# Filling the block-diagonal state matrix: copies on GpSimd from rows already on chip, in place of transfers from memory

## The chip, the core and the metric

The kernel runs on one core of a Trainium2 chip. The metric is the device time of one launch in microseconds (us); lower is better. TensorE does matrix products and transposes, VectorE (DVE in the profile), ScalarE (ACT) and GpSimd (POOL) do elementwise work, and SyncE (SP) issues most of the transfers between the main memory and the core's own memory. All five run at the same time, each through a queue of its own in a fixed order, and wait for each other through semaphores.

## What is computed

Three stages follow one another. The change lies in the first; the two others appear here because their time follows from it.

```python
def _attn_ref(x, state):                 # x (8, 8, 512, 64), state (8, 8, 32, 64)
    scores = scale * np.matmul(x, state.transpose(0, 1, 3, 2))
    a = softmax(scores)                  # over the 32 state rows
    xread = np.matmul(a, state)
    scores2 = scale * np.matmul(state, x.transpose(0, 1, 3, 2))
    a2 = softmax(scores2)                # over the 512 rows of x
    sread = np.matmul(a2, x)
    return np.concatenate([xread, sread], axis=2)
# then: each of the 4608 rows goes to the best of 8 experts, relu(x @ w1) @ w2, scaled by two gates
# then: ((x @ w1) * (x @ w2)) @ w3 @ w_out
```

The two softmaxes are written out in the reference (subtract the maximum, exponential, divide by the sum plus 1e-9).

## The kernel before, in words

The attention handles the eight batches one after the other. The four steps that matter here are:

- `load_x(b)` (line 323) brings one batch of x, 1 MB, with four transfers on SP's queue. `load_state` (line 337) brings all state rows into `st_n`, once, at the start: partition 32 j + n holds row n of the heads 2 j and 2 j + 1, 64 numbers each, for all batches.
- `softmaxes(b)` (line 524) makes the scores of a batch and both softmaxes. VectorE takes maxima and sums (lines 556 to 590), ScalarE the exponentials (lines 586 and 602), GpSimd normalises (line 593). ScalarE, or VectorE, copies transposed blocks out of TensorE's result memory (`cp`, lines 138 to 140; "any" in its lists lets the framework choose the engine).
- `read(b)` (line 623) multiplies the softmax weights with the state. It needs a block-diagonal matrix: for four heads at once, the rows of head j stand in partitions 32 j to 32 j + 31 and in columns 64 j to 64 j + 63, everything else is zero. That is `st_d` (line 373), for four batches at a time and for even and odd heads (g); 32 columns behind hold gate products (`spread_gates`, line 376). Its products are `pxr` (line 654).
- `load_w_out` and `load_w3` bring weights for a later stage as raw 64-bit words and convert them (`convert`, line 211): ScalarE line 225, VectorE 228, 230 and 233, ScalarE 239, GpSimd 240, in this order. Of w_out's blocks (`wu_raw`) three are loaded at the start.

`st_d` is cleared once by GpSimd (line 374). `spread_state(b, n)` (line 381) fills in the rows of n batches. It is called for batches 0 to 3 at the start (line 391), and for two batches each after `read(1)` and `read(3)` (lines 675 and 686), when the products with the old rows are through. Each call issues eight transfers, one for each head, on the queue that `q_std` names in the list KN: SP's. One moves 32 rows for n batches, in runs of 256 bytes: 32 KB in the first call, 16 KB in the two others.

The order of instructions in each queue is not written by hand. The framework lays out the whole program on an estimated timeline when the kernel is built (line 1570), and each engine takes, of the instructions that are ready by that estimate, the one with the highest priority. Priority follows the program's order, with offsets for the attention's steps:

```python
"u": lambda b: ([(load_w_out(i), split_w_out()) for i in WU[b]]),
"r": lambda b: (read(b), b % 2 == 1 and b < B // 2 and spread(b + B // 2 - 1, 2)),
# KN: 'order': 'xswrguf'; prio for x s u r g w f: 0, 300, 0, 300, 0, -300, 0
```

After the attention the logits of all rows give the routing (`route`, line 728); the experts' rows are gathered and their weights loaded by what it decides, and TensorE works through the experts and the last stage.

Of the kernel before, what the change touches and what calls it, by code (L numbers as in the profile page):

```python
# [52 lines left out]
def tile_attention_moe_bilinear(  # L53
# [20 lines left out]
    nc = tc.nc  # L74
    B, H, S, D = x.shape
    NS = state.shape[2]
# [6 lines left out]
    NJ = H // 2  # L83
# [4 lines left out]
    def kn(name, default):  # L88
        return KN.get(name, default)
# [43 lines left out]
    def eng(name, i, default="any"):  # L133
        v = kn(name, default)
        v = v[i % len(v)] if isinstance(v, list) else v
        return getattr(nc, v)
# [49 lines left out]
    def both(t, *at):  # L186
        return t[0][at], t[1][at]
# [122 lines left out]
    with ExitStack() as c1:  # L310
# [12 lines left out]
        def load_x(b):  # L323

            t = xin.tile([P, H, NC_, D], F32, tag="x", name=f"x{b}")
            for j in range(NJ):
                h = slice(2 * j, 2 * j + 2)
                eng("q_x", j, "sync").dma_start(
                    out=t[:, h].rearrange("p h c d -> p h (c d)"),
                    in_=x[b, h].rearrange("h (p c) d -> p h (c d)", c=NC_),  # L330
                )
            x_t[b] = t


        st_n = one.tile([P, B, 2 * D], F32, name="st_n")
# [33 lines left out]
        nc.scalar.dma_start(out=wg[:, :, 0:E], in_=w_gate.rearrange("(k p) e -> p k e", p=P))  # L369
        nc.scalar.dma_start(out=wg[:, :, E:], in_=w_ogate.rearrange("(k p) e -> p k e", p=P))  # L370
        load_x(1)

        st_d = one.tile([P, B // 2, 2, NJ * D + 2 * E], F32, name="st_d")
        nc.gpsimd.memset(st_d, 0.0)
# [4 lines left out]
                nc.gpsimd.tensor_copy(st_d[:, i : i + n, g, NJ * D :], st_g[:, g, b : b + n])  # L379

        def spread_state(b, n):
            for h in range(H):
                j, g = divmod(h, 2)
                i = b % (B // 2)
                eng("q_std", h, "gpsimd").dma_start(
                    out=st_d[NS * j : NS * (j + 1), i : i + n, g, j * D : (j + 1) * D],
                    in_=state[b : b + n, h].rearrange("b n d -> n b d"),
                )

        load_x(2)  # L390
        spread_state(0, B // 2)


        stT = [one.tile([P, B, P], F32, name=f"stT{o}") for o in range(2)]
        for i in range(0, B, 4):
# [6 lines left out]
            for o in range(2):  # L402
# [4 lines left out]
                        turned[:, j].rearrange("p g d -> p (g d)") if o else st_n[:, i + j, :], ident,  # L407
                    )
                nc.vector.tensor_copy(stT[o][:, i : i + 4, :], t.rearrange("p (j n) -> p j n", j=4))

        def of(g):
            return slice(D * g, D * (g + 1))

        def at(j):
            return slice(NS * j, NS * (j + 1))


        st_g = one.tile([P, 2, B, 2 * E], F32, name="st_g")
# [1 line left out]
        def gate_state():  # L420
            t = [bank((kn("t_psg", "C")*4)[0], f"psg{g}")[:, 0 : B * 2 * E] for g in range(2)]
            for b in range(B):
                for j in range(NJ):
                    for g in range(2):
                        nc.tensor.matmul(
                            t[g][at(j), b * 2 * E : (b + 1) * 2 * E], stT[0][of(g), b, at(j)],
                            wg[of(g), j, :], start=True, stop=True,
                        )
            for g in range(2):
                nc.vector.tensor_copy(st_g[:, g], t[g].rearrange("p (b e) -> p b e", e=2 * E))  # L430
# [93 lines left out]
        def softmaxes(b):  # L524
# [20 lines left out]
            for j in range(NJ):  # L545
                for g in range(2):
                    for e in range(2):
                        nc.tensor.matmul(
                            t[e][at(j), g * S // 2 : (g + 1) * S // 2], stT[e ^ g][of(e), b, at(j)],
                            xT[of(e), 2 * j + g, :], start=True, stop=True,  # L550
                        )
# [123 lines left out]
        def spread(b, n):  # L675
            spread_state(b, n)
            spread_gates(b, n)
# [213 lines left out]
    with ExitStack() as c2:  # L891
# [446 lines left out]
        for n, c in enumerate(ORDER):  # L1338
            if c != "b":
                b = [n + 1] if ORDER[n + 1 : n + 2] == "b" else []  # L1340
# [178 lines left out]
    with tc.If(used > T0):  # L1519
        with ExitStack() as c6:  # L1520
            e2 = Lines(c6.enter_context(tc.tile_pool(name="e2_more", bufs=2, reuse_waits="tile")))
            e4 = Lines(c6.enter_context(tc.tile_pool(name="e4", bufs=2, reuse_waits="tile")))
            n = MAXT - T0
# [50 lines left out]
```

## Time and profile before

| what | value |
|---|---|
| median of 3 runs | 1165.69 us (1165.29 to 1167.22) |
| the profiled execution's own time | 1171.04 us |
| its span, first to last instruction | 1169.1 us |
| TensorE's mean granted clock in it | 0.99 |
| busy in the span: TensorE, VectorE, ScalarE, GpSimd | 1118.7, 664.0, 450.7, 398.2 us |
| transfers of the span | 211.55 MB |

Times of rows count from the start of the span. In a timeline a row reads: start, duration (both us), engine and line, operation, written <- read tensors (buffer numbers left out), shapes, how many instructions the row merges, and in brackets how long the engine was idle before and what ended that. SPq is SyncE's queue of transfer issues: the duration there is the issuing, not the transfer itself.

### The profile page before, as it was taken

How to read it: one execution, taken by the hardware profiler on the slowest of the kernel's cores; microseconds unless marked ns; L12 is line 12 of the kernel's file. 1: busy time of each engine (PE TensorE's matmuls, PEld its weight loads, DVE VectorE, ACT ScalarE, POOL GpSimd, SP SyncE). 2: the span in 40 equal slices, each digit the busy share in tenths (PEclk: the TensorE clock that was granted, in tenths of full speed). 3: DMA queues.
4: the chain of work that ended last, by engine and by line, in shares of the span. 5: the costliest groups of instructions: out<-in, count | busy, mean ns of one | idle time of the engine just before them, and what ended most of it. 6: DMA issues, size and time to landing. Idle time of an engine off the chain costs nothing. (4 is left out here: it accounts for less than half of the span.)

```text
span 1169.1 us, 18224 instructions
## 1 busy us (share of the span) xinstructions
PE 1118.7 (96%) x6880; PEld 982.7 (84%) x6880; DVE 664.0 (57%) x1206; ACT 450.7 (39%) x807; POOL 398.2 (34%) x383
## 2 busy tenths in 40 slices
PE   6888998999999999999999999999999999999995
PEld 4666777999999999987888888898888889889994
DVE  4999787636464546464855547343644545463341
ACT  3778644435454545454413223121412322131121
POOL 2555326114140322132001434623543453344222
PEclk9899999999999999999999999999999999999998
DMA  7786425546566666677414645443544445343431
GB/s 227 223 254 200 160 96 209 201 153 228 187 228 211 215 216 201 233 221 242 158 35 176 248 152 199 171 174 141 205 174 160 156 180 189 135 181 132 184 127 57
DMA packets 85008, 211.55 MB, mean 181 GB/s; under 512 B 12976, under 2 KB 42672, under 8 KB 79920
## 3 DMA queue, kind: packets, MB, share of 16 engines
q1 hardware_dynamic: 62256, 167.53, 42.2%
q10 hardware_dynamic: 17024, 24.42, 5.7%
q0 software_dynamic: 5632, 18.35, 4.5%
q8 instruction: 56, 0.92, 0.3%
q14 instruction: 40, 0.33, 0.1%
HBM read 166.23 MB, written 44.04 MB: 180 GB/s over the span
## 5 line engine op out<-in xcount | busy, mean ns | idle before, releaser
L183 PE MATMUL p<-w_x,w 128*128 128x448 f32 (+1 forms) x1638 | 338.6, 360 | 0.0
L183 PEld LDWEIGHTS p<-w_x,w 128*128 128x128 f32 x1638 | 303.7, 188 | 25.4
L183 PE MATMUL py<-h,w 128*128 128x288 f32 (+1 forms) x1152 | 197.9, 329 | 3.0 <-ACT y L1087 3.0
L183 PE MATMUL ph<-x,w 128*128 128x288 f32 (+2 forms) x1248 | 196.5, 316 | 2.9 <-DVE h L1025 2.7
L183 PEld LDWEIGHTS ph<-x,w 128*128 128x128 f32 x1248 | 179.4, 188 | 15.6 <-DVE h L1025 4.4
L183 PEld LDWEIGHTS py<-h,w 128*128 128x128 f32 x1152 | 173.8, 188 | 19.2 <-ACT y L1087 4.6
L178 DVE TENSOR_TENSOR w<-raw,w 128x1024 fp32r<-128x1024 f32 x80 | 96.9, 1237 | 74.6 <-ACT w L177 72.5
L1434 POOL TENSOR_TENSOR ab<-u,s 128x448 f32<-128x448 f32 (+1 forms) x40 | 47.6, 1189 | 259.3 <-DVE u L1432 170.4
L183 PE MATMUL po<-w_wo,aa 128*128 128x512 f32 x480 | 125.3, 393 | 1.9 <-ACT aa L177 1.0
L183 PEld LDWEIGHTS po<-w_wo,aa 128*128 128x128 f32 x480 | 89.7, 188 | 18.8 <-DVE aa L178 1.7
L177 ACT CAST w<-raw 128x1024 fp32r<-128x1024 f32 x80 | 81.6, 1050 | 51.6 <-DMA raw<-in_moe_w 46.8
L177 ACT CAST ab<-ab 128x384 fp32r<-128x384 f32 (+1 forms) x40 | 19.7, 493 | 184.4 <-POOL ab L1440 174.0
L240 POOL TENSOR_TENSOR wab<-wab,wab_top 128x512 int32<-128x512 int32 x16 | 20.7, 1292 | 179.5 <-DVE wab_top L233 151.5
L183 PE MATMUL po<-w_wo,ab 128*128 128x512 f32 x336 | 79.6, 391 | 0.4 <-DVE o L1466 0.4
L183 PEld LDWEIGHTS po<-w_wo,ab 128*128 128x128 f32 x336 | 62.9, 188 | 13.9 <-DVE o L1466 0.8
L997 POOL DMA_INDIRECT xg<-x_rows,gidx x38 | 45.7, 1202 | 83.3 <-PE pxg L1003 66.7
L1437 DVE TENSOR_TENSOR u<-u,p 128x448 f32<-128x448 f32 (+1 forms) x40 | 24.3, 606 | 84.4 <-PE p L183 84.3
L1438 POOL TENSOR_TENSOR ab<-u,s 128x448 f32<-128x448 f32 (+1 forms) x40 | 48.3, 1208 | 49.2 <-DVE u L1437 49.2
L1025 DVE SCALAR_TENSOR_TENSOR h<-ph,h 128x288 fp32r<-128x288 f32 (+2 forms) x104 | 51.2, 502 | 20.8 <-ACT h L1024 20.3
L1024 ACT ACTIVATE h<-ph 128x288 fp32r<-128x288 f32 (+2 forms) x104 | 44.5, 447 | 42.6 <-PE ph L183 30.8
L183 PE MATMUL pwo<-wu,w3T 128*128 128x512 f32 x192 | 50.2, 411 | 3.4 <-POOL w3T L178 2.9
L1440 POOL TENSOR_TENSOR ab<-ab 128x448 f32<-128x448 f32 (+1 forms) x40 | 48.9, 1222 | 3.1
(291 smaller groups left out, 1441.0 us busy)
## 6 DMA issues: line engine op xcount, KB each, us to landing
w<-w_rows SPq DMA_DIRECT2D x39, 1792.0 KB
raw<-in_moe_w SPq DMA_DIRECT2D x80, 512.0 KB
x<-in_x SPq DMA_DIRECT2D x32, 256.0 KB
w_raw<-in_moe_w SPq DMA_DIRECT2D x16, 512.0 KB
x_rows<-xr SPq DMA_DIRECT2D x32, 256.0 KB
w_rows<-wh_s ACTq DMA_DIRECT2D x32, 256.0 KB
y<-y_T SPq DMA_DIRECT2D x8, 896.0 KB
w_rows<-wh_w ACTq DMA_DIRECT2D x32, 192.0 KB
```

Of the source, the lines that this page charges most:

```text
L177: nc.scalar.copy(hi, src)
L178: (engine or nc.vector).tensor_tensor(lo, src, hi.bitcast(F32), op=ALU.subtract)
L183: m = nc.tensor.matmul(o, l[a], r[b], start=start and i == 0, stop=stop and i == 2)
L240: nc.gpsimd.tensor_tensor(wi, wi, top, op=ALU.add)
L997: gathered = nc.gpsimd.indirect_dma_start(out=x[0:r], out_offset=None, in_=x_rows, in_offset=bass.IndirectOffsetOnAxis(ap=gidx[0:r, t - s0 ...
L1024: nc.scalar.activation(hl[0], src, AF.Relu)
L1025: nc.vector.scalar_tensor_tensor(out=hl[1], in0=src, scalar=0.0, in1=hl[0].bitcast(F32), op0=ALU.max, op1=ALU.subtract)
L1434: gpsimd(b2, u3, s5, op=ALU.add)
L1437: vector(u4, u2, p3, op=ALU.add)
L1438: gpsimd(a2, u4, s5, op=ALU.add)
L1440: gpsimd(ab[:, n : 2 * n], a2, b2, op=ALU.mult)
```

## The change

`spread_state` issues no transfers any more. For each of the four partition blocks GpSimd copies the rows of both heads (g = 0 and 1) of n batches out of `st_n`, which is loaded at the start anyway, into the diagonal blocks of `st_d`: four copies a call in place of eight transfers, twelve in place of 24 in all. A copy has 32 partitions and n x 2 x 64 elements in each. The helpers `of` and `at` move up so that they are defined.

```diff
         st_d = one.tile([P, B // 2, 2, NJ * D + 2 * E], F32, name="st_d")
         nc.gpsimd.memset(st_d, 0.0)
...
         def spread_state(b, n):
-            for h in range(H):
-                j, g = divmod(h, 2)
-                i = b % (B // 2)
-                eng("q_std", h, "gpsimd").dma_start(
-                    out=st_d[NS * j : NS * (j + 1), i : i + n, g, j * D : (j + 1) * D],
-                    in_=state[b : b + n, h].rearrange("b n d -> n b d"),
+            i = b % (B // 2)
+            for j in range(NJ):
+                nc.gpsimd.tensor_copy(
+                    st_d[at(j), i : i + n, :, j * D : (j + 1) * D],
+                    st_n[at(j), b : b + n, :].rearrange("p b (g d) -> p b g d", g=2),
                 )
```

## Rows read from the trace of the kernel before

**Rows 1.** Busy time of each engine by stretch: start:end, engines, granted clock, transfers
```profile
0.00:30.00 30.00, 18.41 (x296) 14.40 (x300) 13.83 (x41) 10.50 (x18) 8.21 (x35) 0.95 0.75 221
30.00:125.00 95.00, 83.09 (x910) 59.35 (x903) 94.47 (x250) 74.23 (x158) 53.19 (x45) 0.96 0.74 227
125.00:1169.10 1044.10, 1017.23 (x5688) 908.97 (x5686) 555.73 (x918) 365.93 (x632) 336.76 (x304) 0.99 0.50 176
```

**Rows 2.** Timeline of ScalarE, 15 to 30 us
```profile
15.90 0.72 ACT L602 ACTIVATE a<-sT,nm 128x512 f32<-128x512 f32 x1 [4.04 <-DVE nm L600]
...
19.32 1.06 ACT L586 ACTIVATE a<-a 128x1024 f32<-128x1024 f32 x1
26.21 0.66 ACT L225 ACTIVATE wu_top<-wu_raw 128x512 f32<-128x512 f32 x1 [5.83 <-DMA wu_raw<-in_moe_w_out]
...
28.58 1.06 ACT L140 COPY a2T<-pa2T 128x512 f32<-128x512 f32 x2
```

**Rows 3.** Timeline of VectorE, 26 to 29 us
```profile
26.90 0.43 DVE L228 TENSOR_SCALAR wu_top<-wu_top 128x512 f32<-128x512 f32 x1 [3.90 <-ACT wu_top L225]
27.25 0.17 DVE L589 TENSOR_SCALAR s<-s 128x32 f32<-128x32 f32 x1
28.16 0.43 DVE L228 TENSOR_SCALAR wu_top<-wu_top 128x512 f32<-128x512 f32 x1 [0.73 <-ACT wu_top L225]
```

**Rows 4.** Timeline of SP's queue, 10 to 21 us
```profile
10.78 5.79 SPq L385 DMA_DIRECT2D st_d<-in_state  x8
...
19.14 1.41 SPq L208 DMA_DIRECT2D wu_raw<-in_moe_w_out  x3
```

**Rows 5.** Waits of SP's queue up to 21 us: total us, times, longest
```profile
SPq L385 <- DMA x<-in_x: 3.5, 8, 0.6
```

**Rows 6.** Stretches as in rows 1; the last three columns: clock, transfer engines' share, GB/s
```profile
15.00:18.50 3.50, 3.50 (x69) 2.92 (x61) 3.13 (x13) 2.48 (x6) 0.00 (x0) 1.00 0.39 69
18.50:26.00 7.50, 4.73 (x51) 3.01 (x49) 3.98 (x12) 1.58 (x2) 0.43 (x2) 1.00 0.97 336
...
28.00:37.00 9.00, 7.15 (x83) 5.90 (x84) 8.85 (x18) 6.35 (x14) 5.48 (x4) 0.50 0.54 142
```

**Rows 7.** GpSimd's copies in the first 30 us by shape: total us, mean ns
```profile
L399 POOL COPY turned<-st_n 128x256 f32<-128x256 f32 x4 | 1.5, 405 | 0.4 <-DMA wg<-in_moe_w_gate 0.4
...
L379 POOL COPY st_d<-st_g 128x64 f32<-128x64 f32 x2 | 0.4, 238 | 9.1 <-DVE st_g L430 9.1
```

**Rows 8.** Timeline of all engines, 5 to 9 us
```profile
6.48 1.09 POOL L399 COPY turned<-st_n 128x256 f32<-128x256 f32 x3
...
8.51 0.85 PE L405 MATMUL pst<-ident,turned 128*128 128x128 f32 x3
```

**Rows 9.** Timeline of all engines, 54 to 56 us
```profile
54.34 0.68 DVE L233 SCALAR_TENSOR_TENSOR wu_top<-wu_raw,wu_top 128x512 int32<-128x512 int32 x1
...
55.16 1.27 POOL L240 TENSOR_TENSOR wu<-wu,wu_top 128x512 int32<-128x512 int32 x1 [3.29 <-ACT wu_top L225]
55.18 1.53 DVE L228 TENSOR_SCALAR wu_top<-wu_top 128x512 f32<-128x512 f32 x1
```

**Rows 10.** VectorE's groups by shape, 30 to 125 us: total us, mean ns, idle before
```profile
L233 DVE SCALAR_TENSOR_TENSOR w_top<-w_raw,w_top 128x512 int32<-128x512 int32 x13 | 11.7, 904 | 0.0
...
L228 DVE TENSOR_SCALAR w_top<-w_top 128x512 f32<-128x512 f32 x14 | 8.6, 612 | 0.0
...
L228 DVE TENSOR_SCALAR wu_top<-wu_top 128x512 f32<-128x512 f32 x6 | 4.7, 781 | 0.0
...
L606 DVE TENSOR_SCALAR r<-s 128x2 f32<-128x2 f32 x6 | 3.5, 586 | 0.0
L589 DVE TENSOR_SCALAR s<-s 128x32 f32<-128x32 f32 x6 | 3.4, 569 | 0.0
```

**Rows 11.** Copies of line 140, 30 to 125 us: ns min/median/max, first and last start
```profile
L140 ACT COPY xT<-pxT x16: 560/580/653, 36.3 to 118.3; 128x512 f32<-128x512 f32 x16
...
L140 DVE COPY xT<-pxT x8: 665/676/692, 36.0 to 117.9; 128x512 f32<-128x512 f32 x8
```

More of the change, by code (lines that the diff above doesn't have):

```diff
@@ L371, in tile_attention_moe_bilinear, with of, at @@
         load_x(1)
+        def of(g):
+            return slice(D * g, D * (g + 1))
+        def at(j):
+            return slice(NS * j, NS * (j + 1))
         st_d = one.tile([P, B // 2, 2, NJ * D + 2 * E], F32, name="st_d")
@@ L409, in tile_attention_moe_bilinear @@
                 nc.vector.tensor_copy(stT[o][:, i : i + 4, :], t.rearrange("p (j n) -> p j n", j=4))
[L411 to L415, printed above, removed]
         st_g = one.tile([P, 2, B, 2 * E], F32, name="st_g")
```

## The prediction, written before the result

> **What bounds the kernel now.** I read the stages first: busy time of each engine over the first 30 us, the next 95 us and the rest [rows 1]. The reader should see three different limits. From 125 us to the end TensorE is busy 1017.23 of 1044.10 us; nothing the change touches lies there, so what the start gains is handed on to the end, because routing, gathers and expert weights all wait for the last logits. From 30 to 125 us VectorE is busy 94.47 of 95.00 us, and ScalarE (74.23) and GpSimd (53.19) are not: VectorE alone sets that stage. In the first 30 us nobody is full, and VectorE works 13.83 us: that stage is bound by waits.
>
> So I looked for the wait that ends last there, in time order on ScalarE [rows 2]. ScalarE stands idle 5.83 us, up to 26.21, for the first raw block of w_out; its two conversion pairs come ahead of the copies of a2T in its queue, and those copies start at 28.58 only. VectorE follows: idle 3.90 us up to 26.90 and 0.73 us up to 28.16, both for ScalarE's conversion [rows 3]. After that it has no gap until 125 us. One late transfer thus holds up the whole pipeline for about 4 us.
>
> Why is it late? On SP's queue [rows 4] the eight transfers into st_d are issued from 10.78 and take 5.79 us; behind them come the fourth x block and, at 19.14, the raw blocks of w_out. The waits of SP's queue [rows 5] say why eight small issues take so long: all eight wait for an earlier x transfer to land, 3.5 us together. The DMA engines [rows 6] show the result: from 15 to 18.5 us they are 0.39 busy and move 69 GB/s, from 18.5 to 26 us 0.97 and 336 GB/s. SP was occupied with 32 KB pieces while the engines ran dry.
>
> **What is removed.** The eight transfers leave SP's queue, and the four x issues and three w_out issues move into their places. They will wait for the same landings, so they can't all go at once: the x block goes from 10.78 on, w_out at about 13.5 to 14 (half of 5.79 later). Bounds for how much sooner the block lands: at most the whole 5.79 us of issue time; at least the DMA engines' idle share of the thin stretch, 3.5 x (1 - 0.39) = 2.1 us. I take 3.8 us: the thin stretch (3.5 us, 0.24 MB, almost all of it the 0.26 MB of small transfers) disappears whole, and some 0.3 us of their data in the microsecond ahead of it (an estimate). ScalarE's wait then ends at 26.21 - 3.8 = 22.4, VectorE's at 23.1, just where its own earlier work ends (26.90 - 3.90 = 23.00). What is late next is still this block, by a hair; the 0.73 us gap stays.
>
> The granted clock was 0.50 (the 1.2 GHz level) from 28 to 37 us, after TensorE's idle time; a shorter gap may spare that. It is worth at most the 0.15 us that VectorE is idle in these 9 us [rows 6]; I count nothing.
>
> The sixteen later transfers (after batches 1 and 3) free SP's queue for stores of xr and loads of w3 and w_out behind them. I cost this at nothing: VectorE has 0.53 us of idle time in that whole stage [rows 1], so earlier loads feed an engine that is full. Without that cover it would help ScalarE, not hurt.
>
> **What is added.** Twelve GpSimd copies on 32 partitions. Nearest rows [rows 7]: 256 elements a partition take 405 ns, 64 take 238 ns. The eight copies of the later calls have 256 elements: 8 x 0.405 = 3.2 us. The first four have 512: 0.405 + 256 x (0.405 - 0.238)/192 = 0.63 us each, 2.5 us in all (ends 4 x 0.24 = 1.0 and 4 x 0.81 = 3.2). That fewer partitions make a copy shorter no row shows.
>
> The first four come ahead of the four "turned" copies in program order and may go ahead of them on GpSimd. The turned copies end at 6.48 + 0.40 = 6.9 for the first half, and their transposes start at 8.51 [rows 8]: 1.6 us of cover, so 0.9 us late (0 to 1.6). I count nothing: VectorE's 0.73 us gap behind the big wait takes up nearly all of it. Worst end: 1.6 us.
>
> The eight others sit in VectorE's full stage. Each call's copies wait until batch 1's (3's) products with the old st_d are through; GpSimd's gate copies wait there for the same matmuls already, so the wait is not new, but the normalisations and integer adds queued behind get up to 1.6 us later per call. GpSimd is idle 41.8 of 95 us there, and nobody waits for it that sets the stage; VectorE does not.
>
> What they may cost is VectorE's own time. At 55.18 VectorE starts a tensor_scalar 0.02 us after GpSimd starts an add of 1.27 us; it takes 1.53 us where an undisturbed one took 0.43 [rows 3, 9]. So the two exclude each other in part. How much on average? The five groups of [rows 10] against their undisturbed durations in [rows 3, 9] (0.68 for the two-input form, 0.43 for L228, 0.17 for the small ones) lose 13 x 0.22 + 14 x 0.18 + 6 x 0.35 + 6 x 0.42 + 6 x 0.40 = 12.4 us, that is 0.23 us per us of GpSimd work (53.19). For 3.2 us more: 0.8 us. Ends: 0 and 3.2 us. The first four meet an almost idle VectorE.
>
> The Trainium skill, page "SBUF — State Buffer", section "Who interferes with whom", speaks against the change: VectorE's two-port forms and two-input forms exclude a GpSimd operation through an exclusive lock, and whoever comes second is blocked for the whole instruction. The single pair above agrees; the mean over the stage is far below it. By that rule taken to its end the sum would be that of the first rival below.
>
> **The sum.** 3.8 gained, 0.8 lost: 3.0 us. The profiled execution took 1171.04 us (span 1169.1), 5.35 above the median; I subtract the same 3.0 from both: 1168.0 for it, 1162.7 for the median 1165.69. Two runs of this kernel can be told apart from about 0.2% on, 2.3 us.
>
> **Rivals.**
> (1) *Every new copy costs VectorE its full length.* For: the pair at 55.18. Against: 0.23 on average. 3.8 - 3.2 = 0.6 gained: 1165.1, no change.
> (2) *The planner moves the conversion forward.* Order on each engine is fixed at build from an estimated timeline. It put w_out's conversion ahead of a2T, though that has the higher priority, so it believes the block lands early; with the small transfers gone it will believe in a still earlier landing. If the conversion goes ahead of ScalarE's big exponential (19.32), the pairs run from 22.4 to 24.8 (28.58 - 26.21 = 2.4), and VectorE reaches the point of 28.5 (the end of the second conversion's first step) at 24.8 + (23.0 - 19.3) = 28.5: nothing gained, 0.8 lost, 1166.5, no change.
> (3) *The same, further, and slower than before.* If it goes ahead of the first exponentials (15.90), into ScalarE's idle time before them (4.04 us), the exponentials start at 24.8, and VectorE reaches that point at 24.8 + (23.0 - 15.9) = 31.9, 3.4 late; with the lock 4.2: 1169.9. It decides as soon as the planner's landing time falls before the end of that gap; 26.21 is 10 us behind it, which speaks against.
> (4) *Copies drift to VectorE.* Copies out of PSUM that any engine may make are nearly all on ScalarE: 16 of 24 xT copies, though only one in four is tied to VectorE [rows 11]. If a new plan gives eight more to VectorE, at 0.68 us: 5.4 lost against 3.0 gained, 1168.1, slower. Nothing but the new plan speaks for it.
>
> **Chances.** My forecast holds with 0.54; its own range, by the ends 5.79 and 2.1 of the gain, is 1159.9 (no lock cost) to 1164.4; 0.45 of it lies over 0.2% below the median before, 0.09 within. Rivals 1 and 2 have 0.12 and 0.11, both within 0.2%; rival 3 has 0.13 and rival 4 0.10, both slower. So faster 0.45, same 0.32, slower 0.23. The range 1159.5 to 1168.8 takes in all but rival 3.
>
> **What would show it.** Right: w_out's raw blocks issued before 15 us, no thin stretch in the DMA engines, ScalarE's wait ending near 22.4 and VectorE's long gap gone, VectorE's full stage beginning and ending 3 to 4 us sooner. The copies should read 0.6 us in the first call and 0.4 to 0.7 in the others, and the five groups of [rows 10] some 0.8 us more in sum. Wrong: a landing of w_out's block later than 24 us (the bytes were the limit), a conversion queued ahead of the exponentials, or more copies on VectorE than before.

## The result and the profile after

| what | before | after |
|---|---|---|
| median, runs of both on one chip | 1166.45 us (1165.29 to 1169.63) | 1177.62 us (1177.03 to 1178.93) |
| ratio of the times, 95% interval | | 1.0093 (1.0070 to 1.0116) |
| the profiled execution's own time, its span | 1171.04, 1169.1 us | 1177.03, 1174.9 us |

The change costs 11 us; the forecast was a gain of 3.0. The profiled execution of before is a long one of its kind and that of after a short one, so their spans differ by 5.8 us only. To place the loss I compare single instructions in the two traces.

I began with ScalarE, where the prediction had begun [rows 2]. The timeline of ScalarE after, 10 to 36 us:

```profile
10.31 0.58 ACT L140 COPY xT<-pxT 128x512 f32<-128x512 f32 x1 [1.02 <-PE pxT L531]
20.91 0.66 ACT L225 ACTIVATE wu_top<-wu_raw 128x512 f32<-128x512 f32 x1 [10.02 <-DMA wu_raw<-in_moe_w_out]
...
22.15 0.72 ACT L601 ACTIVATE a<-sT,nm 128x512 f32<-128x512 f32 x1
...
27.98 1.04 ACT L585 ACTIVATE a<-a 128x1024 f32<-128x1024 f32 x1
...
35.22 0.59 ACT L140 COPY a2T<-pa2T 128x512 f32<-128x512 f32 x1 [0.17 <-PE pa2T L613]
```

The raw block of w_out lands 5.3 us sooner (20.91 for 26.21), and yet everything else is later. Its conversion now stands ahead of the first exponentials in ScalarE's queue: ScalarE waits 10.02 us for the block, and the exponentials behind it start at 22.15 instead of 15.90, the big one at 27.98 instead of 19.32, the copies of a2T at 35.22 instead of 28.58. VectorE's timeline shows the same from its side:

```profile
15.52 0.15 DVE L560 TENSOR_TENSOR m<-m2e 128x2 f32<-128x2 f32 x1
21.61 0.43 DVE L228 TENSOR_SCALAR wu_top<-wu_top 128x512 f32<-128x512 f32 x1 [5.94 <-ACT wu_top L225]
21.95 0.16 DVE L599 TENSOR_SCALAR nm<-m 128x2 f32<-128x2 f32 x1
...
22.41 0.68 DVE L579 TENSOR_REDUCE m<-pS 128x16 f32<-128x512 f32 x1
...
32.40 0.41 DVE L555 TENSOR_SCALAR_CACHE_REDUCE sT<-psT 128x256 f32<-128x256 f32 x1
```

VectorE idles 5.94 us where it idled 3.90 [rows 3]: its own part of the conversion stands ahead of nm (21.95), the last input of the exponentials, which needs only the maxima of 15.52. Then the conversions go ahead of the softmax here too: between 21.61 and 32.40 ten of their instructions (lines 228, 230, 233 and 178, 6.38 us together) run before batch 1's first scores at 32.40; before the change those scores came at 21.55, ahead of all of them. So the steps that lead to the end wait for work that nobody needs soon.

The queue of SP and GpSimd's copies did what the change says. SP's queue up to 15 us (start, time for issuing), then GpSimd's copies by shape, up to 125 us:

```profile
3.58 8.99 SPq L328 DMA_DIRECT2D x<-in_x  x16
12.95 1.84 SPq L208 DMA_DIRECT2D wu_raw<-in_moe_w_out  x3
```

```profile
L390 POOL COPY st_d<-st_n 32x256 f32<-32x256 f32 x8 | 3.5, 431 | 0.2
...
L390 POOL COPY st_d<-st_n 32x512 f32<-32x512 f32 x4 | 2.4, 605 | 0.2
...
L404 POOL COPY turned<-st_n 128x256 f32<-128x256 f32 x4 | 1.5, 393 | 0.1
```

The stretches, with the columns of [rows 1, 6]:

```profile
0.00:30.00 30.00, 16.44 (x208) 12.30 (x208) 13.20 (x31) 11.53 (x21) 12.75 (x38) 0.84 0.78 244
30.00:125.00 95.00, 85.34 (x962) 61.24 (x963) 93.10 (x249) 71.01 (x153) 54.14 (x53) 0.94 0.64 210
...
15.00:18.50 3.50, 1.90 (x44) 1.60 (x40) 0.67 (x2) 0.00 (x0) 0.00 (x0) 1.00 1.11 372
18.50:26.00 7.50, 1.60 (x10) 1.26 (x11) 4.39 (x11) 5.07 (x11) 1.27 (x1) 0.61 0.50 182
```

From 15 to 18.5 us the transfer engines move 372 GB/s instead of 69: the thin stretch is gone, as hoped. But in the same 3.5 us VectorE works 0.67 us instead of 3.13 and ScalarE not at all.

How the loss travels is read from five landmarks, starts in us from the span's start. The table has all kernels of this study; what e1 to e11 are follows below.

| kernel | first exponential (ScalarE) | batch 2's first scores (VectorE) | routing's maximum, mx (VectorE) | first py, an expert's second product (TensorE) | first po, last stage (TensorE) |
|---|---|---|---|---|---|
| before | 15.90 | 42.78 | 146.31 | 225.21 | 647.03 |
| after | 22.15 | 50.25 | 152.29 | 234.67 | 653.06 |
| e1 | 16.12 | 41.50 | 151.80 | 229.47 | 648.15 |
| e2 | 16.71 | 35.61 | 153.20 | 235.78 | 658.85 |
| e3 | 23.32 | 49.05 | 155.90 | 234.83 | 652.44 |
| e4 | 21.54 | 48.35 | 154.68 | 232.05 | 655.69 |
| e5 | 16.57 | 38.16 | 141.85 | 220.78 | 641.90 |
| e6 | 19.64 | 41.15 | 143.79 | 221.70 | 641.29 |
| e7 | 26.22 | 54.33 | 159.30 | 241.88 | 661.59 |
| e8 | 15.73 | 41.92 | 148.12 | 230.88 | 649.30 |
| e9 | 15.87 | 37.44 | 139.95 | 219.04 | 636.56 |
| e10 | 15.03 | 41.34 | 143.92 | 221.33 | 643.30 |
| e11 | 17.76 | 39.51 | 142.14 | 220.26 | 640.10 |

After is 6.3 us late at the first exponential, 7.5 at batch 2, 6.0 at the routing, and 9.5 at the first py. VectorE's busy and idle time on the way to the routing's maximum show what the lateness consists of (us; e5 and e7 follow below):

| kernel | busy, idle up to batch 2's first scores | busy, idle from there to mx |
|---|---|---|
| before | 26.15, 16.63 | 96.91, 6.62 |
| after | 32.05, 18.20 | 91.28, 10.76 |
| e5 | 25.96, 12.20 | 94.61, 9.08 |
| e7 | 32.07, 22.26 | 90.51, 14.46 |

Up to mx VectorE works as long in after as before (123.3 and 123.1 us). Of the 7.5 us at batch 2, 5.9 are work done ahead of its time and 1.6 are idle; the work done ahead is saved later, but 4.1 us of new idle time take its place, most of it waits for TensorE's products of the last batch:

```profile
129.67 0.43 DVE L555 TENSOR_SCALAR_CACHE_REDUCE sT<-psT 128x256 f32<-128x256 f32 x1 [1.33 <-PE psT L547]
...
133.57 0.69 DVE L579 TENSOR_REDUCE m<-pS 128x16 f32<-128x512 f32 x1 [2.03 <-PE pS L575]
...
143.73 0.29 DVE L638 TENSOR_TENSOR sr<-psr,r 128x128 f32<-128x128 f32 x1 [0.97 <-PE psr L631]
```

(Timeline of VectorE in after, 125 to 152 us; before waits for none of these three on the way to its mx from 118 us on.) Up to the routing the loss is idle time, not added work.

The last 3.5 us come on TensorE between mx and the first py. It waits 4.0 us for gathered rows (waits, 189 to 206 us; then TensorE's timeline from 200 us on):

```profile
PE pxg L1002 <- DMA xg<-x_rows,gidx: 4.0, 2, 3.0
```

```profile
200.86 0.87 PE L1002 MATMUL pxg<-ident,xg 128*128 128x128 f32 x4 [3.02 <-DMA xg<-x_rows,gidx]
201.39 4.47 PE L183 MATMUL pwo<-wu,w3T 128*128 128x512 f32 x12
205.69 0.64 PE L183 MATMUL ph<-x,w 128*128 128x256 f32 x4
...
208.51 2.49 PE L183 MATMUL pwo<-wu,w3T 128*128 128x512 f32 x10
...
223.05 11.78 PE L183 MATMUL ph<-x,w 128*128 128x256 f32 x96 [1.63 <-DVE h L1024]
```

Before, the same ten products of w_out (pwo) stand ahead of the first ph:

```profile
197.67 2.69 PE L183 MATMUL pwo<-wu,w3T 128*128 128x512 f32 x10
...
200.55 0.72 PE L183 MATMUL ph<-x,w 128*128 128x256 f32 x4
```

Counted from mx, the first ph of after is 0.8 us sooner than before; from there to the first py it takes 29.0 us instead of 24.7, with the ten pwo and a wait of 1.63 us for h in between. From the routing's maximum to the first py take 82.4 us in after and 82.6 to 82.8 in e2, e7 and e8, the kernels in which pwo still runs after the first ph; in all others 77.4 to 79.1. From the first py to the first po the kernels take 417.5 to 423.6 us (before 421.8, after 418.4), and that follows neither the order nor the copies; it is why only 6.0 of the 9.5 us are left at the first po of this pair.

### The profile page after: what moved, and what is told of

It is laid out like the page before. It is cut to its first block, busy times and chain, and to the rows that moved or that the text cites. A ratio compares the mean times of both kernels' runs of the same rounds, so it can differ in the third digit from the quotient of the medians.

```text
span 1174.9 us, 18201 instructions
## 1 busy us (share of the span) xinstructions
PE 1124.7 (96%) x6880; PEld 986.6 (84%) x6880; DVE 665.5 (57%) x1206; ACT 449.9 (38%) x807; POOL 401.3 (34%) x395
## 5 line engine op out<-in xcount | busy, mean ns | idle before, releaser
L183 PEld LDWEIGHTS py<-h,w 128*128 128x128 f32 x1152 | 173.8, 188 | 18.5 <-ACT y L1086 3.9
L183 PEld LDWEIGHTS po<-w_wo,aa 128*128 128x128 f32 x480 | 89.7, 188 | 18.5 <-DVE aa L178 1.6
L996 POOL DMA_INDIRECT xg<-x_rows,gidx x38 | 43.3, 1140 | 87.7 <-PE pxg L1002 81.6
```

The costliest lines, as they stand in the source:

```text
L183: m = nc.tensor.matmul(o, l[a], r[b], start=start and i == 0, stop=stop and i == 2)
L996: gathered = nc.gpsimd.indirect_dma_start(out=x[0:r], out_offset=None, in_=x_rows, in_offset=bass.IndirectOffsetOnAxis(ap=gidx[0:r, t - s0 ...
```

## The experiments

**Theory A**: the loss is the new order of the queues. The framework lays out the program anew when it is built; without the transfers on SP's queue it places the conversion of w_out ahead of the first exponentials. **Theory B**: the copies themselves cost it, as work that VectorE's operations and GpSimd's queue wait for. Each expectation stands as it was written before its run; each ratio is to runs of before on the same chip.

### e1 and e2: the conversion held back

The changed kernel, with one condition: the conversion of batch 0's blocks is queued on ScalarE behind the big exponential of batch 0 (e1) or of batch 1 (e2).

```diff
-            nc.scalar.activation(av, av, AF.Exp, scale=SCALE)
+            big[b] = nc.scalar.activation(av, av, AF.Exp, scale=SCALE)
...
+        def out_weights(b):
+            with tc.issue_after(big[0].ins) if b == 0 else ExitStack():    # e2: big[1]
+                for i in WU[b]:
+                    load_w_out(i)
+                    split_w_out()
...
-            "u": lambda b: ([(load_w_out(i), split_w_out()) for i in WU[b]]),
+            "u": lambda b: out_weights(b),
```

> The changed kernel with one addition: on ScalarE the conversion of the first three w_out blocks is queued behind the big exponential of batch 0, where it stood before the change. The twelve copies on GpSimd stay. Theory A (the new order of the queues costs the time: the conversion, ahead of the first exponentials, holds them until its block lands at 20.9 us): the first exponentials start at 15 to 17 us again, the block still lands near 21, and the median is 1160 to 1167 us. Theory B (the copies on GpSimd cost the time, by holding up VectorE or GpSimd's own queue): 1175 to 1179 us, as with the change alone.

> The changed kernel with the conversion of the first three w_out blocks queued behind the big exponential of batch 1 on ScalarE, so that no engine waits for the block in the first two batches. Theory A: no wait for the w_out block of over 1 us on ScalarE before 30 us, VectorE's full stage starts 4 us or more sooner than before the change, median 1159 to 1166 us. Theory B: 1175 to 1179 us.

Measured: e1 1172.67 us, ratio 1.0042 (1.0026 to 1.0058); e2 1182.69 us, 1.0133 (1.0113 to 1.0152). ScalarE's timeline of e1, then of e2:

```profile
16.12 0.72 ACT L601 ACTIVATE a<-sT,nm 128x512 f32<-128x512 f32 x1 [5.00 <-DVE nm L599]
...
20.41 0.67 ACT L225 ACTIVATE wu_top<-wu_raw 128x512 f32<-128x512 f32 x1
```

```profile
28.08 1.05 ACT L585 ACTIVATE a<-a 128x1024 f32<-128x1024 f32 x1
29.04 0.66 ACT L225 ACTIVATE wu_top<-wu_raw 128x512 f32<-128x512 f32 x1
```

In e1 the start is mended: the block is not waited for at all, and batch 2 begins 1.3 us before that of the kernel before. With twelve copies inside, the ratio falls from 1.0093 to 1.0042, between the ranges of the two theories. But the rest of the gain is lost between batch 2 and the routing, which takes 110.3 us instead of 103.5. e2 misses both: batch 2 begins at 35.61, sooner than in any other kernel, and yet the routing is later than after's. Each edit made the framework lay out all later batches anew, so neither run isolates the start. The last step of w3's conversion on VectorE (line 233) starts at 142.50 in before, 151.69 in after, 147.98 in e1 and 152.60 in e2; whether holding the first conversion back put it there in e1 and e2 is not shown.

### e3: no copies, the transfers on another queue

The kernel before, with `q_std` set to GpSimd's queue: 24 transfers as before, no copies, SP's queue free of them.

```diff
- 'q_std': 'sync',
+ 'q_std': 'gpsimd',
```

> The kernel before with the 24 small transfers issued by GpSimd's queue and not by SP's: SP's queue is as free as with the change, but there is no copy on GpSimd. In this build the conversion again stands ahead of the first exponentials on ScalarE. Theory A: as slow as the change, 1173 to 1181 us, with the first exponentials at 20 us or later. Theory B: no copies, so 1160 to 1168 us.

Measured: 1178.02 us, 1.0103 (1.0072 to 1.0134). ScalarE's timeline:

```profile
22.21 0.66 ACT L225 ACTIVATE wu_top<-wu_raw 128x512 f32<-128x512 f32 x1 [10.67 <-DMA wu_raw<-in_moe_w_out]
...
23.32 0.71 ACT L602 ACTIVATE a<-sT,nm 128x512 f32<-128x512 f32 x1
```

The whole loss without one copy, and the same order on ScalarE with a wait of 10.67 us. For that order at the start it is enough that the transfers leave SP's queue. GpSimd is no freer here than with copies: issuing the first eight transfers takes it 4.60 us (the four copies of after 2.4).

### e4: copies in the first call only

The changed kernel, but the two later calls issue the eight transfers again.

```diff
         def spread(b, n):
-            spread_state(b, n)
+            spread_moved(b, n)        # the eight transfers of the kernel before
```

> The changed kernel with copies in the first call alone (four); the two later calls issue their small transfers on SP's queue as before. In this build the conversion stands ahead of the first exponentials. Theory A: 1174 to 1180 us, since the order at the start is the changed one. Theory B: the eight copies in VectorE's full stage are gone, so most of the loss is too: 1164 to 1170 us.

Measured: 1177.32 us, 1.0069 (1.0045 to 1.0094). The conversion stands ahead of the first exponential again (20.31 and 21.54). Most of the loss is there with the first call's edit alone. The intervals of this ratio and of the change's own overlap and the later order differs too, so what the later copies add can't be read from this pair.

### e5 to e7: copies and order told apart

To hold the order still, I wrote it down. Every instruction of the attention gets an edge without a semaphore to its predecessor on its engine, by a list taken from the build of the other kernel; copies "any" go where they went there. The copies (or transfers) of `spread_state` are left out of the list and placed by the framework. So is the program behind the attention: the list ends before the routing and the experts, though the expectations name them.

```diff
+        traced = [i for i in nc.cur_bb.bb.instructions if i.name not in moved]
+        for row in ORDERS:                       # one row of positions for each of the five engines
+            for a, b in zip(row, row[1:]):
+                tc.add_manual_dep(
+                    traced[b], traced[a].name,
+                    mybir.DependencyInfo(mybir.DependencyClass.NoSync, mybir.DependencyReason.DATA),
+                    reason="order",
+                )
```

e5: copies with the order of before. e6: the same, and each of the twelve copies is made twice (`for _ in range(2):` around it). e7: transfers with the order of after.

> The changed kernel (twelve GpSimd copies, no small transfers), with the order of the kernel before written down for all five engines throughout the attention, the routing and the start of the experts. Theory A (the new order costs the time): with the old order the blind forecast should come true, three stages unchanged, the raw block of w_out landing near 21 us, the first exponential back near 15.9 us, the last softmax batch starting 2 to 4 us before that of the kernel before: 1161 to 1166 us, ratio 0.995 to 1.000. Theory B (the copies cost it, through VectorE's lock or GpSimd's queue): the order changes little, 1174 to 1179 us, ratio 1.006 to 1.011.

> As e5, and every one of the twelve copies is made twice, so that GpSimd has another 5.7 us of work. Theory A: by 0.23 us of VectorE per us of GpSimd in VectorE's full stage, 0.8 us later than e5 (0 to 3.2 us), ratio at most 0.003 above that of e5. Theory B: the price of the copies once more, 8 to 11 us later than e5.

> The kernel before (24 small transfers on SP's queue, no copies), with the order of the changed kernel written down for all five engines throughout the attention, the routing and the start of the experts. Theory A: as slow as the changed kernel or slower, because the conversion of w_out again stands ahead of the first exponentials and its block lands later, near 26 us: 1177 to 1184 us, ratio 1.010 to 1.016. Theory B: without copies the time stays that of the kernel before, 1164 to 1168 us, ratio 0.998 to 1.002.

Measured, as ratios to before:

| | order of before | order of after |
|---|---|---|
| 24 transfers | 1 (before, 1167.42 us) | e7: 1.0150 (1.0132 to 1.0167), 1184.60 us |
| 12 copies | e5: 0.9965 (0.9950 to 0.9979), 1163.79 us | after: 1.0093 (1.0070 to 1.0116) |

The table speaks for theory A. In either order the copies are faster than the transfers, by 0.35% and by some 0.6%; in either form the new order costs 1.3 to 1.5%. The change alone gains 4.1 us (2.5 to 5.8), against a forecast of 3.0, and the reordering takes back over three and a half times that. Neither kernel was run with its own order written down, so what the edges alone do to the time was not measured; e10 below, old order with the first call's transfers, comes within 0.15% of before. ScalarE of e5, the stretch from 15 to 18.5 us, and VectorE's waits from 20 to 45 us:

```profile
16.57 0.72 ACT L611 ACTIVATE a<-sT,nm 128x512 f32<-128x512 f32 x1 [4.04 <-DVE nm L609]
...
22.12 0.66 ACT L233 ACTIVATE wu_top<-wu_raw 128x512 f32<-128x512 f32 x1 [1.07 <-DMA wu_raw<-in_moe_w_out]
...
24.54 1.05 ACT L148 COPY a2T<-pa2T 128x512 f32<-128x512 f32 x2
```

```profile
15.00:18.50 3.50, 3.50 (x99) 2.73 (x88) 3.13 (x14) 1.93 (x6) 0.00 (x0) 1.00 1.11 369
```

```profile
DVE s L597 <- ACT a L595: 0.5, 1, 0.5
```

That is the picture the prediction drew: the block at 22.12 (forecast 22.4), the copies of a2T 4.0 us sooner than in [rows 2], no wait of VectorE for the conversion, and 4.4 to 4.6 us gained at batch 2, the routing and the first py alike. By batch 2 the gain is idle time (16.63 to 12.20 us); behind it 2.3 us less of busy and 2.5 us more of idle time cancel. In e7 the same order meets transfers, the block comes later, and the wait is the longest of all:

```profile
24.99 0.66 ACT L233 ACTIVATE wu_top<-wu_raw 128x512 f32<-128x512 f32 x1 [13.48 <-DMA wu_raw<-in_moe_w_out]
...
26.22 0.72 ACT L612 ACTIVATE a<-sT,nm 128x512 f32<-128x512 f32 x1
```

e6 missed: 1169.08 us, 1.0015 (1.0003 to 1.0027), 0.0050 above e5, where theory A allowed 0.003. Its timelines of GpSimd and VectorE show why:

```profile
7.42 1.90 POOL L400 COPY st_d<-st_n 32x512 f32<-32x512 f32 x3
...
10.07 0.40 POOL L415 COPY turned<-st_n 128x256 f32<-128x256 f32 x1
```

```profile
17.75 0.42 DVE L566 TENSOR_SCALAR_CACHE_REDUCE sT<-psT 128x256 f32<-128x256 f32 x1 [0.90 <-PE psT L558]
```

Eight copies now run ahead of the turned copies, which begin at 10.07 (e5: 7.46, before: 5.34, with the three others at 6.48 [rows 8]). TensorE's transposes wait for them, and VectorE's first scores come at 17.75 instead of e5's 14.67. The profile does not carry this to the end: it is of e6's fastest execution (1164.69 us), and the 3.0 us at batch 2 have shrunk to 0.9 at the first py and are gone at the first po.

### e8: copies in the later calls only

The kernel before, with its first call as it was and eight copies in the two later calls; the order is the framework's.

```diff
-        spread_state(0, B // 2)
+        spread_moved(0, B // 2)       # transfers; spread_state itself makes the copies
```

> The first call with the eight small transfers as before, the two later calls with eight GpSimd copies, order chosen by the framework; the order of the first 30 us stays that of the kernel before. Theory A: within a few us of the kernel before, 1163 to 1170 us, ratio 0.998 to 1.004, and what differs goes with a changed order of the later batches. Theory B: most of the loss, since eight of the twelve copies and all that meet a full VectorE are in it: 1172 to 1178 us, ratio 1.005 to 1.010.

Measured: 1173.65 us, 1.0061 (1.0041 to 1.0080), as theory B had it. The start is that of before (first exponential 15.73, batch 2 at 41.92); 2.7 us are lost between batch 2 and the routing, and 3.9 more up to the first py. That could be the copies or another new order, and e10 was made for that.

### e9 to e11: place and number of the copies

All three have the order of before written down. e9: as e5, but the first four copies stand behind the turned copies in GpSimd's queue. e10: e8 with that order. e11: as e5, with the eight later copies alone made twice.

```diff
         load_x(2)
-        spread_state(0, B // 2)
...
+        spread_state(0, B // 2)       # e9: after the setup, with an edge from the last turned copy
         softmaxes(0)
```

> As e5 (twelve copies, the order of the kernel before), but the first four copies stand behind the four turned copies in GpSimd's queue instead of ahead of them. If the first call's place in GpSimd's queue costs what e5's start shows (turned copies at 7.46 instead of 5.34 us, first scores on VectorE at 14.67 instead of 14.00), the first scores come back to 14.0 and the whole is about 0.7 us earlier than e5: 1162.5 to 1164 us, ratio 0.995 to 0.9965. If that start is covered by the block of w_out, as the prediction had it (worst end 1.6 us, counted at nothing), the time is that of e5, ratio 0.9965.

> As e8 (first call by eight transfers, eight later GpSimd copies), with the order of the kernel before written down for all five engines. If what e8 lost (ratio 1.006) was a new order of the later batches, it is gone: the time of the kernel before plus 0.8 us for the lock (0 to 3.2), 1166 to 1170 us, ratio 0.999 to 1.002. If the eight copies cost it in VectorE's full stage, it stays: 1172 to 1176 us, ratio 1.004 to 1.008.

> As e5, but only the eight later copies are made twice (3.6 us more GpSimd work in VectorE's full stage, the start left alone). e6, with all twelve twice, ran 0.005 above e5 by the ratio, some 5 us. If that came from the start (the second set of first copies put the turned copies 2.6 us later), this kernel is within 0.8 us of e5: ratio 0.9965 to 0.9975. If it came from the later copies (lock on VectorE, or GpSimd's queue), it stays 3 to 5 us above e5: ratio 0.999 to 1.002.

Measured: e9 1160.85 us, 0.9944 (0.9926 to 0.9962); e10 1166.02 us, 0.9985 (0.9972 to 0.9998); e11 1164.37 us, 0.9979 (0.9961 to 0.9997).

**e10** against e8: the same copies and transfers, 0.0076 apart by order alone, some 9 us. What e8 lost was a new order of the later batches. (The 0.9985 lies just below the 0.999 to 1.002 expected for that.) On ScalarE the block's wait of before is back, since the first call issues its transfers:

```profile
25.31 0.66 ACT L233 ACTIVATE wu_top<-wu_raw 128x512 f32<-128x512 f32 x1 [5.80 <-DMA wu_raw<-in_moe_w_out]
```

**e11**: the later copies in the stretch from 30 to 125 us, twice as many:

```profile
L400 POOL COPY st_d<-st_n 32x256 f32<-32x256 f32 x16 | 8.4, 527 | 0.6
```

That is 4.4 us more GpSimd work than in e5 (eight in 4.0 us), for 0.0014 by the ratios, with intervals that overlap: 1.6 us, and by the two intervals anything between 0 and some 4. The ratio falls between the two expectations, 0.0004 above the first. From batch 2 to the routing e11 takes 102.6 us and e5 103.7; VectorE is busy 95.92 us of it in e11, and 94.61 to 95.70 in e5, e9 and e10, which share order and later copies. By the ratios e6 lies 0.0036 above e11, which differs from it in the first copies alone: by the times, then, most of e6's loss came from the start.

**e9** looks at the start from the other side. GpSimd's timeline, then VectorE's and ScalarE's:

```profile
5.46 0.40 POOL L419 COPY turned<-st_n 128x256 f32<-128x256 f32 x1 [0.56 <-DMA wg<-in_moe_w_gate]
...
7.61 2.56 POOL L399 COPY st_d<-st_n 32x512 f32<-32x512 f32 x4
```

```profile
13.98 0.42 DVE L570 TENSOR_SCALAR_CACHE_REDUCE sT<-psT 128x256 f32<-128x256 f32 x1 [0.90 <-PE psT L562]
```

```profile
21.42 0.66 ACT L233 ACTIVATE wu_top<-wu_raw 128x512 f32<-128x512 f32 x1 [1.07 <-DMA wu_raw<-in_moe_w_out]
```

The turned copies are back at 5.46, the first scores at 13.98 (before 14.00, e5 14.67), and the block is converted at 21.42. By the ratios it is 2.5 us faster than e5 where 0.7 was expected; the two intervals overlap a little, so the surplus isn't established. e9 is faster than both kernels of this case: 6.5 us (4.4 to 8.6) below before, by its ratio.

## Why the prediction was wrong

**The step that failed** is rival 3's dismissal, and with it the unsaid premise of the sum that every queue keeps its order. The prediction named the mechanism (the conversion goes ahead of the first exponentials, into ScalarE's idle time), saw that the order is fixed at build from an estimated timeline, and then weighed it by a measured time: "26.21 is 10 us behind it, which speaks against". By its own account what decides is the landing that the build believes in, and no row shows that. One row hinted at it, and rival 2 had read it so: in the old order w_out's conversion stood ahead of a2T's copies although its block came 5.83 us late [rows 2], which suggests that the estimate was too early by several us already. The 0.13 given to it was too little for a program in which any edit is followed by a new layout.

**Its size.** Rival 3 had the exponentials at 24.8 and VectorE 3.4 us late. They came at 22.15, because the block landed sooner and only one pair of conversions went first. But the loss did not end with that one wait: VectorE, given conversions ahead of softmax steps, was 7.5 us late at batch 2, idled 4.1 us more from there to the routing, and TensorE lost 3.5 us more up to the first py, with ten pwo behind the first ph. No step of the prediction looked there.

**The landing of w_out.** Forecast 3.8 us sooner (2.1 to 5.79): 5.3 in after, 4.1 in e5. w_out's issues went at 12.95 in after, 14.09 in e5 (forecast 13.5 to 14), and the thin stretch was gone in both. Right, with the term somewhat small.

**The copies' price.** 0.63 and 0.405 us forecast: 0.605 and 0.431 in after; the eight later ones took 0.501 on average in e5. Right, or 0.1 us low. Fewer partitions do not make a copy shorter: 32 partitions with 256 elements take 431 ns where 128 take 393.

**The first call at nothing.** Wrong by its cover: the 0.73 us gap that was to hide the delay is one of the two waits that the change removes. The turned copies begin 2.1 us late (7.46 in e5, 7.49 in e11; 5.34 to 5.54 in before, e8, e9 and e10). What that costs is not established: the first scores are 0.67 us late in e5, and e9 gives 0.69 back, but single executions with the same order and first call differ there by 0.87 (e10, 13.13, against before) and 1.19 (e11, 15.86, against e5).

**The lock, 0.8 us.** Not seen and not excluded. In e5 none of the five groups of [rows 10] has a higher mean than before (the two-input form 831 ns against 904, L228's 580 against 612). The Trainium skill, page "SBUF — State Buffer", section "Who interferes with whom", has the second comer blocked for the whole instruction; taken to its end the later copies made twice would have cost all of 4.4 us. e11's 1.6 us (0 to 4) lies below that, but the times alone hardly exclude it. Nor do the traces price it: from batch 2 to the routing VectorE's busy time is 96.91 us in before, without a copy there, and spreads by 1.1 us over e5, e9 and e10, more than the 0.8 in question.

**Rivals 1, 2 and 4.** Rival 1's 1165.1 us would be a ratio of 0.9995, above e5's interval. Rival 2 was a milder form of what happened. Rival 4 did not: from 30 to 125 us ScalarE makes 16 of the xT copies and VectorE 8, as in [rows 11].

**What stays open** is how the framework's estimate comes to that landing; no trace shows it. That the order at the start followed from taking the transfers off SP's queue, and needs no copies, is shown by e3; that the order cost the time, by e5, e7 and e10.

## What to carry to other kernels

Where a framework fixes the order of the queues from an estimate, an edit has two effects, its own and that of the new layout, and the second can be several times the first; before trusting a sum, ask which ready-but-unneeded work could be put ahead of a step on the path if its input is believed early. When a sound change comes out slower, compare the order of instructions on each engine first, then run the change with the old order held and the old kernel with the new one: four numbers tell change and order apart. And place added work by its due time, not by where it stands in the source: the first copies were needed only at the first `read`, at 30.84 us in e5, and ran from 3.59 on.

## What the runs showed that I had not expected

The granted clock fell where the pipeline stalled. From 28 to 37 us it was 0.50 before (the 1.2 GHz level [rows 6]). With the order of after it is 0.61 from 18.5 to 26 us, when TensorE works 1.60 of 7.50 us, and 0.50 again from 28 to 37; in e5 and e9, where ScalarE waits 1.07 us for the block, it reads 1.00 all through the first 30 us and from 28 to 37:

```profile
0.00:30.00 30.00, 20.27 (x344) 15.93 (x345) 18.49 (x49) 13.06 (x24) 15.40 (x42) 1.00 0.76 237
30.00:125.00 95.00, 86.11 (x927) 60.84 (x929) 93.98 (x256) 74.44 (x161) 52.41 (x50) 1.00 0.70 224
```

(Stretches of e9, columns as in [rows 1].) It is not the block's wait alone: e6 and e11 read 1.00 for the first 30 us, too, but 0.81 from 28 to 37. I counted nothing for it. What part of e5's and e9's gain is the clock's was not separated. And the small transfers cost more by where they were issued than by what they moved, 0.52 MB in all: with the same bytes on GpSimd's queue, in e3, w_out's issues go at 14.46 instead of 19.14 and the block is converted at 22.21 instead of 26.21.
